# Two layers of sliding-window attention and MLP for one token: adding the quadrants of each head's output once a group instead of once a head

## The chip, the cores and the metric

The kernel runs on 1 core of one Trainium2 chip. The metric is the device time of one execution, in microseconds (us); three runs of the kernel before gave 519.72, 519.97 and 520.18, median 519.97.

## The reference, cut to what matters

Two layers are computed, each with an attention block A and an MLP block B, for one token with D = 640. A has 32 heads of Dh = 192, each with its own keys and values, of which only the last W = 4096 positions count. Both layers read the same caches and weights.

```python
def A(x):
    q = (x @ wq).reshape(1, 1, 32, 192).transpose(0, 2, 1, 3)
    k, v = k_cache[:, :, Sk - W:, :], v_cache[:, :, Sk - W:, :]
    p = softmax(einsum("bhqd,bhkd->bhqk", q, k) * 192 ** -0.5)
    o = einsum("bhqk,bhkd->bhqd", p, v)
    return o.transpose(0, 2, 1, 3).reshape(1, 1, 6144) @ wo
...
x = x + A(layernorm(x))
x = x + B(layernorm(x))     # B: gelu(ln @ w1), shifted, @ w2; gelu(ln @ w3) @ w4
x = x + A(layernorm(x))
x = x + B(layernorm(x))
```

For a single token the shifts of B move in only zeros, so w1 and w2 don't count: B(x) = x + gelu(layernorm(x) @ w3) @ w4.

## The kernel before, in words

A head's K and V are 4096 x 192 bf16, 1.5 MB each, and go into cells: 11 tiles of 12288 bytes on each of 128 partitions. `need(key)` issues, on SyncE's queue (SP), the loads of a fixed order (`layer_stream`) up to the one asked for. Each takes a cell (`take`) that `give` has put back, first in, first out, and its issue waits until the last reader of that cell is done. wq stays in SBUF. Of layer 0's keys, those of heads 0 to 6 stay transposed in cells (NKEEP = 7, `kept`), with the V of head 3 and parts of two others, so that layer 1 need not load them; so the cells that go round become fewer towards the end of layer 0. There w3 and w4 also take cells.

The heads go in 8 groups of 4 (QH); layer 0 from the last group to the first, layer 1 from the first to the last. In `attention`, a group `gi` runs like this:

- K of a head is transposed in four quarters by VectorE in blocks of 32 x 32 words (L377, `T(h, half)` for two quarters), and TensorE forms its scores in two halves (L453, `S(h, half, ...)`).
- The group's softmax is cut into steps (`softmax_steps`): part_max (VectorE), turn_max (TensorE), full_max (VectorE), spread_max (TensorE, then ScalarE's exponential with the row sum), turn_p, swap, recip. Between them stand the transposes and scores of the next group's first two heads, the projection of the q's two groups on (`q[0]` to `q[3]`) and the output projection of the group before (`pending`; either `out_proj`, columns, L597, or `out_row`, rows, L615).
- Then, head by head, `pv` (L569) multiplies V by the probabilities: 16 matmuls write 4 quadrants of PSUM rows, two rows each, with 2 x 192 columns. VectorE turns the result into `o_sb` (L576), an SBUF tile whose bytes also hold the probabilities of the softmax (`o_bytes`).
- Behind each `pv` come the transposes and scores of a later head of the next group, and then `o_fold` (L578 to L589) adds the quadrants: matmuls in fp32 with `Lq` (128 x 32, four unit matrices one below the other) write the head's 192 numbers as 32 x 6, and ScalarE scales them by 1/sum into 32 rows of `oT`. In two groups of layer 1 and four of layer 0, VectorE first adds the two row halves (L587) and one matmul does (L588); in the others two matmuls do (L583). An fp32 matmul shows as two records in the profile.

The next to last group (`hurry`) does the whole softmax of the last group between its own heads. In the last group (`final`), no next group's scores are left: after head 0's `pv` layer 0 projects the `pending` group, then `add_y` adds it; after head 1 `center_y` takes the mean off; the folds of heads 2 and 3 are put off, the one of head 2 into the middle of the next `pv` and that of head 3 behind it. Then the last group is projected and `mixer` (B) follows: two matmuls with `ones` sum the row (L866, L868), w3's columns (L901), gelu, w4's (L933).

`ones` is a 128 x 128 fp32 tile of ones (L264); as the stationary operand of a matmul it adds over partitions and puts the sum on every one (L325, L338, L528, L681, L866, L868). Ahead of the first work on x stand 66 small matmuls into a tile that nobody reads (L308 to L310). All PSUM tiles named psm share a ring of two buffers. The order on TensorE, VectorE, ScalarE and SyncE is that of the program.

Of the kernel before, what the change touches and what calls it, by code (L numbers as in the profile page):

```python
# [17 lines left out]
P = 128  # L18
# [17 lines left out]
def kernel(  # L36
# [37 lines left out]
    NA = Dh // 32  # L74
    NKX = 6
    NKEEP, NCELL = 7, 11
    WARM = 66

# [182 lines left out]
        out=ident[:], in_=ident[:], compare_op=ALU.not_equal, fill=1.0,  # L261
        base=0, pattern=[[-1, P]], channel_multiplier=1,
    )
    ones = const.tile([P, P], F32, name="ones")  # L264
    nc.vector.memset(ones[:], 1.0)
    Lf = wx_sb[:, 0:2 * P].bitcast(F32).rearrange("p (j i) -> p j i", j=4)
    nc.gpsimd.memset(Lf, 0.0)
    for base in (0, -1, -64, -65):
# [20 lines left out]
    blkm = head.tile([P, NM], F32, name="blkm")  # L289
    nc.vector.reduce_sum(blkm[:], ident[:].rearrange("p (m b) -> p m b", m=NM), axis=AX.X)  # L290

    Lq = const.tile([P, 32], F32, name="Lq")
    nc.vector.reduce_sum(Lq[:], ident[:].rearrange("p (j a) -> p a j", j=4), axis=AX.X)
    eps1 = head.tile([P, 1], F32, name="eps1")
    nc.vector.memset(eps1[:], eps)

# [8 lines left out]
    nc.gpsimd.memset(Qblk[:], 0.0)  # L305


    warm_ps = psm.tile([32, 32], F32, tag="psm")  # L308
    for i in range(WARM):
        nc.tensor.matmul(warm_ps[:], lhsT=Eq[:, 0, :], rhs=Eq[:, 0, :], start=(i == 0), stop=(i == WARM - 1))  # L310

    x_rf = wx_sb[0:ND, 6 * P:8 * P].bitcast(F32)
    nc.vector.tensor_copy(x_rf, x_bf)
    xT = const.tile([P, ND], F32, name="xT0")
# [7 lines left out]
    def ln_center(x, rowsum):  # L322

        mean_ps = psm.tile([P, 1], F32, tag="psm")
        nc.tensor.matmul(mean_ps[:], lhsT=ones[:], rhs=rowsum[:, 0:1], start=True, stop=True)  # L325
        xc = big.tile([P, ND], BF16, name="xc")
        nc.vector.scalar_tensor_tensor(out=xc[:], in0=mean_ps[:, 0:1].broadcast_to([P, ND]), scalar=-1.0 / D,
                                       in1=x[:], op0=ALU.mult, op1=ALU.add)
        xcf = big.tile([P, ND], F32, name="xcf")
        nc.vector.scalar_tensor_tensor(out=xcf[:], in0=mean_ps[:, 0:1].broadcast_to([P, ND]), scalar=-1.0 / D,  # L330
                                       in1=x[:], op0=ALU.mult, op1=ALU.add)
        junk = sm.tile([P, ND], F32, tag="ln_junk")
        ssq = sm.tile([P, 1], F32, tag="ln_ssq")
        nc.scalar.activation(junk[:], xcf[:], ACTF.Square, accum_out=ssq[:, 0:1])

        def total():
            var_ps = psm.tile([P, 1], F32, tag="psm")
            nc.tensor.matmul(var_ps[:], lhsT=ones[:], rhs=ssq[:, 0:1], start=True, stop=True)  # L338
            return var_ps

        return xc, xcf, total
# [131 lines left out]
    def softmax_steps(n, ST_ps, sc):  # L473
# [25 lines left out]
        def spread_max():  # L499
            nb_ps = psm.tile([P, 1], F32, tag="psm")  # L500
            nc.tensor.matmul(nb_ps[:], lhsT=held["w"],  # L501
                             rhs=ones[0:1, 0:1], start=True, stop=True)
# [14 lines left out]
        def swap():  # L517
            ng = NGK // NT
            PT_ps = psm.tile([P, n, NJ4, NGK], F32, tag="psm")
            src = held["PrT"].rearrange("p (g j i) -> p i j g", g=ng, j=NJ4)  # L520
            for m in range(NM):
                for q in range(NT):
                    nc.tensor.matmul(PT_ps[32 * m:32 * (m + 1), :, :, ng * q:ng * (q + 1)], lhsT=Eq[:, q, :],  # L523
                                     rhs=src[:, m:QW:NM], start=True, stop=True)
            PT = big.tile([P, n, NJ4 * NGK], BF16, name="PT")
            nc.scalar.copy(PT[:].rearrange("p h c -> p (h c)"), PT_ps[:].rearrange("p h j g -> p (h j g)"))  # L526
            l_ps = psm.tile([P, QH], F32, tag="psm")
            nc.tensor.matmul(l_ps[:], lhsT=ones[:], rhs=held["lh"][:], start=True, stop=True)  # L528
            held["lps"] = l_ps
            return PT  # L530

# [43 lines left out]
            give(("v", layer, h))  # L575
        nc.vector.transpose(o_sb[:], O_ps.rearrange("p (e a c) -> p e c a", e=2, c=NA))  # L576

    def o_fold(h, oT, rl, add=False):  # L578
        r = slice(32 * (h % QH), 32 * (h % QH) + 32)
        oT_ps = psm.tile([P, NA], F32, tag="psm")  # L580
        if not add:
            for e in range(2):
                nc.tensor.matmul(oT_ps[r, :], lhsT=Lq[:], rhs=o_sb[:, e, :, e], start=(e == 0), stop=(e == 1))  # L583
            nc.scalar.activation(oT[r, :], oT_ps[r, :], ACTF.Copy, scale=rl[r, 0:1])  # L584
            return
        o2 = sm.tile([P, NA], F32, name="o2")
        nc.vector.tensor_add(o2[:], o_sb[:, 0, :, 0], o_sb[:, 1, :, 1])  # L587
        nc.tensor.matmul(oT_ps[r, :], lhsT=Lq[:], rhs=o2[:], start=True, stop=True)  # L588
# [52 lines left out]
    def attention(layer, x_cur, rs_cur, x_new, z_new, rs_new, ss_new):  # L641
# [29 lines left out]
        def add_y(y_ps, n):  # L671
            y_new = x_new if n == 0 else sm.tile([P, ND], F32, name="y_acc")
            if n == 1:
# [4 lines left out]

                def center():
                    nm_ps = psm.tile([P, 1], F32, tag="psm")  # L680
                    nc.tensor.matmul(nm_ps[:], lhsT=ones[:], rhs=rs[:, 0:1], start=True, stop=True)  # L681
# [52 lines left out]
        for gi, cur in enumerate(groups):  # L734
            nxt = list(enumerate(groups[gi + 1])) if gi + 1 < len(groups) else []
            ST_n = None
            if nxt:
# [24 lines left out]
                else:  # L762
# [5 lines left out]
                    part_max()  # L768
                    T(h0, 1)
                    S(h0, 0, ST_n, 0)  # L770
                    turn_max()
                    full_max()
                    S(h0, 1, ST_n, 0)
# [32 lines left out]
            hurry = gi + 2 == len(groups)  # L806
            final = gi + 1 == len(groups)
            fold = None
            order = list(enumerate(cur))
# [44 lines left out]
            last = (cur[0] // QH, oT)  # L854
            if not final:
                pending = last
            ST = ST_n
        add_y(out_proj(layer, last) if layer == 0 else out_proj(layer, pending, last), 0)

    def mixer(layer, x_cur, z, rs_cur, ss_cur, x_new, rs_new):  # L860
# [2 lines left out]


        s1_ps = psm.tile([P, 1], F32, tag="psm")
        nc.tensor.matmul(s1_ps[:], lhsT=ones[:], rhs=rs_cur[:, 0:1], start=True, stop=True)  # L866
        s2_ps = psm.tile([P, 1], F32, tag="psm")
        nc.tensor.matmul(s2_ps[:], lhsT=ones[:], rhs=ss_cur[:, 0:1], start=True, stop=True)  # L868
# [119 lines left out]
```

## Time and profile before

| what | value |
|---|---|
| median of three runs | 519.97 us |
| the profiled execution's own time | 519.84 us |
| its span, first to last instruction | 518.0 us |
| TensorE busy (weight loads) | 324.8 us, 63% (192.6 us, 37%) |
| VectorE busy | 295.2 us, 57% |
| ScalarE busy | 49.5 us, 10% |
| read from HBM | 216.47 MB |
| mean TensorE clock granted | 0.70 |
| K transposes, L377 | 228 of 945 ns |
| scores, L453 | 1536 of 380 ns |
| P.V, L569 | 1018 of 461 ns |
| o's transpose, L576 | 64 of 581 ns |

A page of the profile gives, for each engine, the time it was busy, and for each line of the kernel the number of instructions, their busy time, the mean of one, the idle time of the engine right before them and what ended most of it. The timeline gives single instructions by their start. SPq is SyncE's queue of DMA issues; "us to landing" counts from issue until all bytes have arrived. The windows give the same sums for stretches of the span, with the share of TensorE's clock that was granted, the mean busy share of the 16 DMA engines and the bytes moved a second. Busy time of an engine counts only where nothing else is late: the prediction asks for each step what comes last there.

### The profile page before, as it was taken

What the parts mean: (1) busy time and instruction counts of PE and PEld (TensorE: products, weight loads), DVE (VectorE), ACT (ScalarE), POOL (GpSimd) and SP (SyncE); (2) the same over time, 40 slices, a digit from 0 to 9 for tenths busy, and PEclk for the clock granted to TensorE, in tenths of its full rate; (3) what the DMA queues carried; (4) which work ended last, traced back from release to release, by engine and by line L of the source; (5) the groups of instructions that cost most, each with busy time, mean ns of one, the idle gap of its engine ahead of it and who ended that gap; (6) DMA issues with size and microseconds to landing.
All of it is one profiled execution on the core that took longest, in us unless ns stands there. A gap on an engine that the chain in (4) does not pass through costs nothing.

```text
span 518.0 us, 9589 instructions
## 1 busy us (share of the span) xinstructions
PE 324.8 (63%) x4146; PEld 192.6 (37%) x4146; DVE 295.2 (57%) x589; ACT 49.5 (10%) x175; POOL 4.0 (1%) x16
## 2 busy tenths in 40 slices
PE   2057656666664566767755866777566856648665
PEld 2024334333332334434333634434333433425334
DVE  2067667575584655656624356567675765664722
ACT  1000101010010100001011111001010101001011
POOL 2000000000000000000000000000000000000000
PEclk9999878565586755677665778557785676776855
DMA  8999999999999999999999999999999999999995
GB/s 347 433 425 426 433 426 427 432 428 425 433 426 427 431 426 429 428 426 431 424 425 396 385 426 429 428 428 428 429 426 427 432 428 426 426 434 426 427 416 235
DMA packets 23949, 217.08 MB, mean 419 GB/s; under 512 B 2532, under 2 KB 3044, under 8 KB 8420
## 3 DMA queue, kind: packets, MB, share of 16 engines
q1 hardware_dynamic: 23908, 216.48, 99.0%
q8 instruction: 32, 0.52, 0.4%
q14 instruction: 9, 0.07, 0.0%
HBM read 216.47 MB, written 0.00 MB: 418 GB/s over the span
## 4 chain that ended last, share of the span: by engine, by line
DMA 50%; PE 23%; DVE 22%; issue 2%; ACT 1%; SPq 1%; DVEq 0%; ACTq 0%
DMA cell<-in_A_k_cache_dram 39%; DVE cell L377 16%; DMA cell<-in_A_v_cache_dram 9%; PE ST_ps L453 9%; PE O_ps L569 7%; DVE o_sb L576 2%; DMA cell<-in_B_w_dram 2%; DVE pm L478 1%; PE nb_ps L501 1%; DVE o_sb L512 1%; ACT o_sb L507 1%; PE y_ps L637 1%; PE l_ps L528 1%; PE PT_ps L523 1%; PE qT_ps L407 1%
## 5 line engine op out<-in xcount | busy, mean ns | idle before, releaser
L453 PE MATMUL ST_ps<-cell,Qblk 128*16 128x256 bf16 x1536 | 163.7, 380 | 106.9 <-DVE cell L377 69.4
L377 DVE STREAM_TRANSPOSE cell<-cell 128x768 uint32<-128x768 uint32 x228 | 204.1, 945 | 15.2 <-DMA cell<-in_A_k_cache_dram 14.9
L453 PEld LDWEIGHTS <-Qblk 128*16 128x16 bf16 x1536 | 86.1, 111 | 176.5 <-issue 150.3
L569 PE MATMUL O_ps<-cell,PT 128*2 128x384 bf16 x1018 | 99.9, 461 | 8.2 <-DMA cell<-in_A_v_cache_dram 7.4
L576 DVE STREAM_TRANSPOSE o_sb<-O_ps 128x384 f32<-128x384 f32 x64 | 37.2, 581 | 111.8 <-PE O_ps L569 111.6
L569 PEld LDWEIGHTS <-PT 128*2 128x2 bf16 x1024 | 46.0, 100 | 22.1 <-issue 10.1
L512 DVE STREAM_TRANSPOSE o_sb<-o_sb 128x256 bf16<-128x256 bf16 x16 | 7.1, 446 | 33.2 <-ACT o_sb L507 24.2
L584 ACT ACTIVATE oT<-oT_ps,rl 32x6 bf16<-32x6 f32 x40 | 10.3, 258 | 164.0 <-PE oT_ps L583 157.8
L583 PEld LDWEIGHTS oT_ps<-o_sb,Lq 128*32 128x32 f32 x160 | 13.3, 145 | 19.3 <-issue 15.8
L583 PE MATMUL oT_ps<-o_sb,Lq 128*32 128x6 f32 x160 | 13.9, 195 | 10.4 <-DVE o_sb L576 9.9
L589 ACT ACTIVATE oT<-oT_ps,rl 32x6 bf16<-32x6 f32 x24 | 6.2, 258 | 107.6 <-PE ST_ps L453 87.1
L407 PE MATMUL qT_ps<-xc,wq_sb 128*128 128x1 bf16 x210 | 7.1, 165 | 12.8 <-DMA wq_sb<-in_A_wq_dram 12.0
L523 PE MATMUL PT_ps<-o_sb,Eq 128*32 128x32 bf16 x256 | 7.3, 237 | 9.3 <-DVE o_sb L512 4.1
L523 PEld LDWEIGHTS <-Eq 128*32 128x32 bf16 x256 | 5.4, 108 | 19.8 <-issue 19.7
L421 DVE TENSOR_TENSOR Xq<-qT_ps,maskq 128x24 bf16<-128x24 f32 (+1 forms) x18 | 2.8, 158 | 17.1 <-PE qT_ps L407 17.1
L396 PE MATMUL qr_ps<-wq_sb,xc 128*1 128x384 bf16 x90 | 12.1, 415 | 0.0
L407 PEld LDWEIGHTS <-wq_sb 128*128 128x128 bf16 x210 | 6.7, 102 | 14.0 <-DMA wq_sb<-in_A_wq_dram 13.0
L504 ACT COPY nb_sb<-nb_ps 128x1 f32<-128x1 f32 x16 | 2.5, 159 | 94.6 <-PE nb_ps L501 94.6
L615 PE MATMUL yr_ps<-cell,oT 128*1 128x320 bf16 x108 | 11.2, 355 | 0.0
L528 PE MATMUL l_ps<-lh,ones 128*128 128x4 f32 x32 | 7.7, 310 | 4.9 <-ACT PT L526 4.9
L428 PE MATMUL Qrep_ps<-Xq,Lb 128*128 128x24 bf16 (+1 forms) x18 | 3.2, 178 | 11.1 <-DVE Xq L421 10.8
L588 PE MATMUL oT_ps<-o,Lq 128*32 128x6 f32 x48 | 6.1, 199 | 6.5 <-DVE o L587 6.5
(143 smaller groups left out, 200.9 us busy)
## 6 DMA issues: line engine op xcount, KB each, us to landing
cell<-in_A_k_cache_dram SPq DMA_DIRECT2D x57, 1536.0 KB, 26.3
cell<-in_A_v_cache_dram SPq DMA_DIRECT2D x57, 1536.0 KB, 25.8
cell<-in_A_wo_dram SPq DMA_DIRECT2D x13, 960.0 KB, 26.5
wq_sb<-in_A_wq_dram SPq DMA_DIRECT2D x5, 1536.0 KB, 12.2
cell<-in_A_v_cache_dram SPq DMA_DIRECT2D x4, 768.0 KB, 23.8
cell<-in_A_v_cache_dram SPq DMA_DIRECT2D x2, 1248.0 KB, 11.5
cell<-in_B_w_dram SPq DMA_DIRECT2D x1, 1536.0 KB, 11.9
cell<-in_B_w_dram SPq DMA_DIRECT2D x2, 768.0 KB, 10.3
```

What stands on the lines that cost most here:

```text
L377: nc.vector.transpose(Tu, Ku[:, :, q * NY:(q + 1) * NY])
L396: nc.tensor.matmul(qr_ps[32 * i:32 * i + 1, :], lhsT=xc[:, kc:kc + 1], rhs=wq_sb[:, kc, t0 * P + i * N:t0 * P + (i + 1) * N], start=(kc == ...
L407: nc.tensor.matmul(qT_ps[:, tl:tl + 1], lhsT=wq_sb[:, kc, t * P:(t + 1) * P], rhs=xc[:, kc:kc + 1], start=(kc == 0), stop=(kc == ND - 1))
L453: nc.tensor.matmul(ST_ps[r:r + QW, :].rearrange("p (g i) -> p g i", g=ng), lhsT=Q[:, n, :], rhs=T4[:, :, f, :, t], start=(hq == 0 and n == ...
L512: nc.vector.transpose(held["PrT"], held["Pr"])
L523: nc.tensor.matmul(PT_ps[32 * m:32 * (m + 1), :, :, ng * q:ng * (q + 1)], lhsT=Eq[:, q, :], rhs=src[:, m:QW:NM], start=True, stop=True)
L528: nc.tensor.matmul(l_ps[:], lhsT=ones[:], rhs=held["lh"][:], start=True, stop=True)
L569: nc.tensor.matmul(O_ps[r:r + 2, :], lhsT=PT[:, hq, 2 * i:2 * i + 2], rhs=v_pair(V, h, 2 * i * Dh, 2 * Dh), start=(i < 4), stop=(i >= NB - 4))
L576: nc.vector.transpose(o_sb[:], O_ps.rearrange("p (e a c) -> p e c a", e=2, c=NA))
L583: nc.tensor.matmul(oT_ps[r, :], lhsT=Lq[:], rhs=o_sb[:, e, :, e], start=(e == 0), stop=(e == 1))
L584: nc.scalar.activation(oT[r, :], oT_ps[r, :], ACTF.Copy, scale=rl[r, 0:1])
L615: nc.tensor.matmul(yr_ps[32 * i:32 * i + 1, :], lhsT=oT[:, k:k + 1], rhs=wo_t[:, k * D + i * N:k * D + (i + 1) * N], start=(k == 0), stop= ...
```

## The change

- In all groups but the last of each layer, VectorE adds the two row halves of every head right behind o's transpose (`o_add`), into a row block of `o4` (128 x 4 x 6). `o_fold` is no longer called there.
- One fp32 matmul a group (`group_fold`), with `L4` (four copies of `Lq` side by side, 128 x 128), adds the quadrants of all four heads and puts each head's numbers on all four blocks of rows; four ScalarE activations scale them into `oT`. It stands in the next group behind the first half of its first head's scores (`pending_fold`), and for the next to last group behind the first P.V of the last one.
- In layer 0's last group the projection of the pending group moves from behind head 0's P.V to behind head 1's, and `center_y` from behind head 1's to behind head 2's. The last group of each layer keeps `o_fold`, with two matmuls a head.
- `ones` becomes a column of ones, read with step 0 as 128 x 128.
- The 66 matmuls at the start go, and `L4` takes four reductions at the start instead of one.

```diff
-    WARM = 66
...
-    ones = const.tile([P, P], F32, name="ones")
-    nc.vector.memset(ones[:], 1.0)
+    one = const.tile([P, 1], F32, name="one")
+    nc.vector.memset(one[:], 1.0)
+    ones = one[:, 0:1].broadcast_to([P, P])
...
-    Lq = const.tile([P, 32], F32, name="Lq")
-    nc.vector.reduce_sum(Lq[:], ident[:].rearrange("p (j a) -> p a j", j=4), axis=AX.X)
+    L4 = const.tile([P, P], F32, name="L4")
+    Lq = L4[:, 0:32]
+    for j in range(4):
+        nc.vector.reduce_sum(L4[:, 32 * j:32 * j + 32], ident[:].rearrange("p (j a) -> p a j", j=4), axis=AX.X)
...
-    warm_ps = psm.tile([32, 32], F32, tag="psm")
-    for i in range(WARM):
-        nc.tensor.matmul(warm_ps[:], lhsT=Eq[:, 0, :], rhs=Eq[:, 0, :], start=(i == 0), stop=(i == WARM - 1))
...
-    def o_fold(h, oT, rl, add=False):
+    def o_fold(h, oT, rl):
         r = slice(32 * (h % QH), 32 * (h % QH) + 32)
         oT_ps = psm.tile([P, NA], F32, tag="psm")
-        if not add:
-            for e in range(2):
-                nc.tensor.matmul(oT_ps[r, :], lhsT=Lq[:], rhs=o_sb[:, e, :, e], start=(e == 0), stop=(e == 1))
-            nc.scalar.activation(oT[r, :], oT_ps[r, :], ACTF.Copy, scale=rl[r, 0:1])
-            return
-        o2 = sm.tile([P, NA], F32, name="o2")
-        nc.vector.tensor_add(o2[:], o_sb[:, 0, :, 0], o_sb[:, 1, :, 1])
-        nc.tensor.matmul(oT_ps[r, :], lhsT=Lq[:], rhs=o2[:], start=True, stop=True)
+        for e in range(2):
+            nc.tensor.matmul(oT_ps[r, :], lhsT=Lq, rhs=o_sb[:, e, :, e], start=(e == 0), stop=(e == 1))
         nc.scalar.activation(oT[r, :], oT_ps[r, :], ACTF.Copy, scale=rl[r, 0:1])
+
+    def o_add(h, o4):
+        nc.vector.tensor_add(o4[:, h % QH, :], o_sb[:, 0, :, 0], o_sb[:, 1, :, 1])
+
+    def group_fold(o4, oT, rl):
+        oT_ps = psm.tile([P, QH, NA], F32, tag="psm")
+        nc.tensor.matmul(oT_ps[:].rearrange("p h c -> p (h c)"), lhsT=L4[:], rhs=o4[:].rearrange("p h c -> p (h c)"),
+                         start=True, stop=True)
+        for i in range(QH):
+            r = slice(32 * i, 32 * i + 32)
+            nc.scalar.activation(oT[r, :], oT_ps[r, i, :], ACTF.Copy, scale=rl[r, 0:1])
...
                     S(h0, 0, ST_n, 0)
+                    if pending is not None:
+                        pending_fold()
                     turn_max()
...
                 pv(layer, h, hq, PT, fold)
+                if not final:
+                    o_add(h, o4)
                 if final:
-                    if layer == 0 and hq == 0:
+                    if hq == 0:
+                        pending_fold()
+                    if layer == 0 and hq == 1:
                         add_y(out_proj(layer, pending), 1)
-                    if hq == 1:
+                    if hq == 2 - layer:
                         center_y()
...
-                o_fold(h, oT, rl, len(groups) - 4 > gi >= 2 * layer)
                 if hurry and hq == 3:
...
                 pending = last
+
+                def pending_fold(o4=o4, oT=oT, rl=rl):
+                    group_fold(o4, oT, rl)
```

More of the change, by code (lines that the diff above doesn't have):

```diff
@@ L324, in ln_center @@
         mean_ps = psm.tile([P, 1], F32, tag="psm")
-        nc.tensor.matmul(mean_ps[:], lhsT=ones[:], rhs=rowsum[:, 0:1], start=True, stop=True)
+        nc.tensor.matmul(mean_ps[:], lhsT=ones, rhs=rowsum[:, 0:1], start=True, stop=True)
         xc = big.tile([P, ND], BF16, name="xc")
@@ L337, in total @@
             var_ps = psm.tile([P, 1], F32, tag="psm")
-            nc.tensor.matmul(var_ps[:], lhsT=ones[:], rhs=ssq[:, 0:1], start=True, stop=True)
+            nc.tensor.matmul(var_ps[:], lhsT=ones, rhs=ssq[:, 0:1], start=True, stop=True)
             return var_ps
@@ L501, in spread_max @@
             nc.tensor.matmul(nb_ps[:], lhsT=held["w"],
-                             rhs=ones[0:1, 0:1], start=True, stop=True)
+                             rhs=one[0:1, 0:1], start=True, stop=True)
             nb_sb = big.tile([P, 1], F32, name="nb_sb")
@@ L527, in swap @@
             l_ps = psm.tile([P, QH], F32, tag="psm")
-            nc.tensor.matmul(l_ps[:], lhsT=ones[:], rhs=held["lh"][:], start=True, stop=True)
+            nc.tensor.matmul(l_ps[:], lhsT=ones, rhs=held["lh"][:], start=True, stop=True)
             held["lps"] = l_ps
@@ L680, in center @@
                     nm_ps = psm.tile([P, 1], F32, tag="psm")
-                    nc.tensor.matmul(nm_ps[:], lhsT=ones[:], rhs=rs[:, 0:1], start=True, stop=True)
+                    nc.tensor.matmul(nm_ps[:], lhsT=ones, rhs=rs[:, 0:1], start=True, stop=True)
                     ym = big.tile([P, ND], F32, name="y_m")
@@ L808, in attention @@
             fold = None
+            o4 = None if final else big.tile([P, QH, NA], F32, name="o4")
             order = list(enumerate(cur))
@@ L865, in mixer @@
         s1_ps = psm.tile([P, 1], F32, tag="psm")
-        nc.tensor.matmul(s1_ps[:], lhsT=ones[:], rhs=rs_cur[:, 0:1], start=True, stop=True)
+        nc.tensor.matmul(s1_ps[:], lhsT=ones, rhs=rs_cur[:, 0:1], start=True, stop=True)
         s2_ps = psm.tile([P, 1], F32, tag="psm")
-        nc.tensor.matmul(s2_ps[:], lhsT=ones[:], rhs=ss_cur[:, 0:1], start=True, stop=True)
+        nc.tensor.matmul(s2_ps[:], lhsT=ones, rhs=ss_cur[:, 0:1], start=True, stop=True)
         def centred(dt, name):
```

## The prediction

> **What bounds the kernel now.** I read the page's line of DMA share first, then the rate by stretches, then the chain of waits, then the timeline where the rate falls.
>
> The page, busy tenths in 40 slices of 12.95 us, and the queue's share:
>
> ```profile
> DMA  8999999999999999999999999999999999999995
> ...
> q1 hardware_dynamic: 23908, 216.48, 99.0%
> ...
> DMA 50%; PE 23%; DVE 22%; issue 2%; ACT 1%; SPq 1%; DVEq 0%; ACTq 0%
> ```
>
> Every slice but the first and the last is 9: the loads' queue is busy 99.0% of the span, TensorE 63% and VectorE 57%. The chain names PE and DVE for 45%, but it follows a load back to what let it be issued, even if the load then stood behind others, so I don't price edits by it. I take four stretches of the table of windows (columns: length, busy time of PE, weight loads, DVE, ACT, POOL; granted clock; DMA share; GB/s):
>
> ```profile
> 4.00:270.00 266.00, 161.79 (x1888) 93.96 (x1889) 155.57 (x292) 21.59 (x75) 0.00 (x0) 0.72 1.01 428
> 270.00:300.00 30.00, 19.70 (x442) 13.93 (x442) 11.59 (x46) 3.90 (x18) 0.00 (x0) 0.63 0.99 395
> 300.00:490.00 190.00, 127.07 (x1531) 73.21 (x1527) 120.22 (x213) 18.14 (x63) 0.71 (x2) 0.69 1.01 428
> 490.00:518.00 28.00, 16.28 (x291) 11.48 (x291) 7.55 (x37) 4.58 (x19) 0.00 (x0) 0.57 0.81 332
> ```
>
> 456 of the 518 us run at 428 GB/s, and 217.08 MB at 428 take 507.2 us. The other 10.8 us are the start (4 us at 169 GB/s: 2.4 lost), the change of layers (30 x (1 - 395/428) = 2.3 lost) and the end (28 x (1 - 332/428) = 6.3 lost). Nothing done in the two long stretches shortens them; a change can gain at most in the last three.
>
> At the change of layers the queue runs nearly dry twice, at 282 to 286 and at 292 to 296:
>
> ```profile
> 282.00:284.00 2.00, 1.98 (x62) 1.90 (x62) 0.88 (x8) 0.58 (x3) 0.00 (x0) 0.50 0.86 340
> 284.00:286.00 2.00, 0.71 (x27) 0.81 (x28) 1.44 (x10) 1.30 (x6) 0.00 (x0) 0.50 0.94 307
> 292.00:294.00 2.00, 2.00 (x58) 1.30 (x47) 0.15 (x1) 0.46 (x2) 0.00 (x0) 0.91 1.03 340
> 294.00:296.00 2.00, 1.65 (x54) 1.22 (x54) 0.83 (x3) 0.00 (x0) 0.00 (x0) 1.00 0.84 301
> ```
>
> By the same sum they lose 1.0 us each. There the next loads wait for cells that a chain of small steps frees: last V lands (277.06), P.V, o folded, y, mixer (w3's cell free 283.69, w4's about 287), q and scores of layer 1 (first kept cell free 291.01).
>
> **The change, part by part.** The profiled execution took 519.84 us (span 518.0 and 1.84 around it), 0.13 below the median 519.97.
>
> *The folds of 14 groups (seven a layer).* Rows of the groups:
>
> ```profile
> L583 PE MATMUL oT_ps<-o_sb,Lq 128*32 128x6 f32 x160 | 13.9, 195 | 10.4 <-DVE o_sb L576 9.9
> L588 PE MATMUL oT_ps<-o,Lq 128*32 128x6 f32 x48 | 6.1, 199 | 6.5 <-DVE o L587 6.5
> L528 PE MATMUL l_ps<-lh,ones 128*128 128x4 f32 x32 | 7.7, 310 | 4.9 <-ACT PT L526 4.9
> ```
>
> Gone: 128 of the 160 matmuls of L583 (32 heads x 4; the last groups' 8 heads keep theirs), 128 x 0.195 = 25.0 us by single durations (overlapped, 13.9 x 0.8 = 11.1 busy), and all of L588, 6.1 busy. Added: one fp32 matmul a group, two records like L528's, which take 0.59 us together at half clock: 14 x 0.59 = 8.3. TensorE is 9 us less busy. VectorE gets 56 - 24 = 32 more adds of 0.149 us (L587) = 4.8 us, all standing between o's transpose and the next head's K transposes. ScalarE keeps 64 activations, four in a row per group (4 x 0.258 = 1.03 us). They stand ahead of nb_sb's copy, which waits anyway for the second half of scores.
>
> On the compute path a head loses its fold between scores and P.V (0.35 to 0.6 us) and gains 0.15 on VectorE; the group end loses TensorE's wait of 0.78 us for o_sb, and the next group's T is late there instead. The group fold comes after the first half of scores, where TensorE waits for the second half's K transposes (two of 0.945 us and part_max's 0.39 against 1.45 us of scores): the cover is about 0.8 us for 0.59, and without it softmax starts some 0.3 us later. So each group's compute is 1 to 2 us shorter, and this buys nothing, because the groups are paced by landings: 0. If the queue weren't full it would be worth up to 14 x 2 us; the 428 GB/s of the stretches rule that out.
>
> *The pending projection of layer 0's last group moves one head back, and this frees a cell later.* Following takes and gives of the cells: V of head 3, the last V of the layer, sat in the cell that the pending out_proj frees; now it takes head 1's V cell, and w3 gets the projection's. The timeline (SPq rows are issues; in brackets what ended the wait):
>
> ```profile
> 264.45 0.96 PE L597 MATMUL y_ps<-oT,cell 128*128 128x1 bf16 x30
> 264.56 1.28 SPq L145 DMA_DIRECT2D cell<-in_A_v_cache_dram  x3
> ...
> 267.40 1.45 PE L569 MATMUL O_ps<-cell,PT 128*2 128x384 bf16 x16 [1.68 <-DMA cell<-in_A_v_cache_dram]
> ...
> 268.89 0.39 SPq L177 DMA_DIRECT2D cell<-in_B_w_dram  x1
> ...
> 277.06 0.81 PE L569 MATMUL O_ps<-cell,PT 128*2 128x384 bf16 x8 [2.85 <-DMA cell<-in_A_v_cache_dram]
> ```
>
> V 3 was issued by 265.8; now it waits for head 1's P.V, which a landing holds at 267.40, and goes at 268.89 where w3 went; w3, queued on SP behind it, about 1 us later, when the projection ends. Is 268.89 too late? The four wq loads that TensorE waits for arrive at 10.63, 14.29, 17.99 and 21.63, 3.67 us apart. So the first, issued at 0.75 into an empty queue, landed near 6.97: 6.2 us from issue, 3.67 of streaming and 2.5 fixed. V 3 lands at 277.06, so an issue up to 270.9 holds it: 2.0 us to spare. Taken: 0; bound +0.7 (the sixteen engines don't run level, and the rate already sags a little at 271).
>
> The group fold there (0.59) and four activations stand behind head 0's P.V; TensorE then waits 1.68 us for V 1. The projection and its add go where it waits 1.98 us for V 2; center_y where it waits 2.85 us for V 3. In layer 1's last group the fold is covered downstream by waits for loads of 0.61, 0.58, 0.23 and 0.89 us up to w3's second half at 511.10; if they were gone it would cost 0.6.
>
> *ones becomes one column read 128 times with step 0.* No row shows such a weight load. Nearest: L866's 128x128 fp32 load, 0.31 us. Below it could cost as little as L483's load (0.08), above I allow twice, so -0.23 to +0.31 a load. Between 277 and 291 two matmuls (s1 and mean, two loads each) lie on the chain that frees cells: -0.9 to +1.2 us. Still 128 columns are loaded, so I take 0. At the end w3's landing hides it.
>
> *No warm-up.* 66 matmuls, 1.9 us at 4.28, with TensorE waiting for wq until 21.63: 0. The first scores at 27.13 took 1.44 us per half, exactly as at 307.71 where the granted clock was 0.50; so the warm-up had left nothing. The Trainium skill ("TensorE: Matmul & The Clock Gate", Why this matters for your kernels) speaks against removing it: 4 us of matmuls keep the array at full clock. By that rule the first scores would be slower without it; the same page's idle window of 3.4 us agrees with the row that they are already slow.
>
> *Setup:* three more reductions of 0.37 us on VectorE ahead of x's cast, which waits 1.08 for x: xc may be ready 0.1 later, and wq's last chunk comes 12 us after. 0.
>
> Sum: 519.84 + 0 = 519.8; the runs' median lies 0.1 higher, so **519.9**.
>
> **Rivals.**
> 1. *Faster through the change of layers.* If the clock there (0.50 until about 292.4) is granted a stretch earlier, the scores of heads 0 and 1 take 0.86 (row at 292.71) instead of 1.46 us each, cells come 1.2 us earlier and the second dip's 1.0 us goes: 518.8. A cheap step-0 load does the same. Against: the change adds hardly any TensorE work between 277 and 292. 12 in 100.
> 2. *Slower: V 3 comes late.* Its issue now hangs on head 1's P.V. From 270.9 on each us is a us on everything after; 0.2% needs 272.0, that is head 1's P.V ending 3.1 us later than now, or step 0 and skew working together. Price then as a dip of today, 1.0 to 1.3: 521.1. 8 in 100.
> 3. *Slower: the step-0 weight load* at twice the price, +1.2 us of chain: 521.1. 6 in 100.
> 4. *The change doesn't free the compute path*, since T takes the place of each fold: also 519.9, inside the forecast.
>
> **How the numbers follow.** About 0.2% (1.04 us) is what a measurement of this kernel tells from no change. Forecast 74 in 100, rival 1 12, rivals 2 and 3 together 14. The bounds -1.0 and +1.2 about 519.9 give 518.8 to 521.1. Faster 0.12, within 0.74, slower 0.14.
>
> **What would show it.** Right: 428 GB/s in both long stretches; SP's issue of V 3 near 268.9 and its P.V still near 277; no wait of TensorE for o_sb at group ends, the same time for T; loads issued earlier after their cells. Wrong: a third dip at 270 to 275; s1 and mean longer than 0.59 us; the clock at full before 290; a rate that isn't 428 when the engines touch memory less.

## The result, and the profile after

| | median | runs | lowest to highest |
|---|---|---|---|
| before | 520.17 us | 22 | 519.52 to 521.96 |
| after | 521.21 us | 22 | 519.75 to 524.64 |

The ratio is 1.0024, 95% interval 1.0014 to 1.0033: slower by 0.24%, 1.0 us. Forecast were 519.9, no change, and 518.8 to 521.1 as bounds. The profiled execution took 521.01 us (span 519.2), 1.2 more than before's.

The page and the table of windows of the kernel after (columns as in the prediction):

```profile
DMA  8999999999999999999999999999999999999995
...
q1 hardware_dynamic: 23908, 216.48, 98.9%
```

```profile
4.00:270.00 266.00, 161.88 (x1753) 89.20 (x1755) 158.83 (x305) 21.57 (x75) 0.00 (x0) 0.71 1.01 428
270.00:300.00 30.00, 20.59 (x436) 14.38 (x434) 11.44 (x48) 3.74 (x17) 0.00 (x0) 0.59 1.00 389
300.00:490.00 190.00, 123.57 (x1440) 69.46 (x1440) 123.61 (x232) 17.50 (x60) 0.71 (x2) 0.69 1.01 428
490.00:519.00 29.00, 17.22 (x306) 11.90 (x306) 8.35 (x41) 5.35 (x22) 0.00 (x0) 0.60 0.81 330
```

Both long stretches still run at 428 GB/s. TensorE's busy time fell by 1.5 us (324.8 to 323.3) and not by the forecast 9: the folds' own rows fell from 20.0 to 11.3 us, but those of P.V rose from 99.9 to 106.1. VectorE's rose from 295.2 to 302.4. The loss is in the change of layers (389 instead of 395) and at the end.

**A third dip.** The 3 us from 270, and the dip of 282 to 286 (340 and 307 GB/s before), in windows of before and then of after:

```profile
270.00:273.00 3.00, 1.04 (x10) 0.23 (x10) 1.02 (x2) 0.26 (x1) 0.00 (x0) 0.50 1.04 431
```

```profile
270.00:273.00 3.00, 1.08 (x14) 0.37 (x13) 0.97 (x4) 0.26 (x1) 0.00 (x0) 0.50 0.91 326
...
282.00:284.00 2.00, 2.00 (x56) 2.00 (x57) 0.89 (x8) 0.53 (x3) 0.00 (x0) 0.50 1.04 412
284.00:286.00 2.00, 0.70 (x27) 0.71 (x25) 1.19 (x8) 1.02 (x5) 0.00 (x0) 0.50 1.10 389
```

326 instead of 431 GB/s is a hole in the stream of loads, the third dip that the prediction named as a sign of being wrong. The old dip behind it, at 282 to 286, has become shallower: part of what the queue would have lost there is already lost at 271. The timeline of after shows who came late:

```profile
264.65 4.75 SPq L144 DMA_DIRECT2D cell<-in_A_v_cache_dram  x3
...
267.58 1.45 PE L567 MATMUL O_ps<-cell,PT 128*2 128x384 bf16 x16 [1.91 <-DMA cell<-in_A_v_cache_dram]
268.96 0.96 PE L600 MATMUL y_ps<-oT,cell 128*128 128x1 bf16 x30
...
269.95 0.39 SPq L176 DMA_DIRECT2D cell<-in_B_w_dram  x1
...
277.51 0.81 PE L567 MATMUL O_ps<-cell,PT 128*2 128x384 bf16 x8 [2.60 <-DMA cell<-in_A_v_cache_dram]
```

V 3 is the V of head 3, the last V of layer 0; V 1 and V 2 are those ahead of it. The row at 264.65 holds three issues; the third, V 3, ends with it at 269.40, behind head 1's P.V, as predicted (268.89). Its P.V starts at 277.51 instead of 277.06.

**Waits that moved.** TensorE's waits over the whole span (us in total, times, longest), first of before, then of after:

```profile
PE ST_ps L453 <- DVE cell L377: 69.4, 76, 3.8
PE ST_ps L453 <- DVE pm L478: 32.3, 13, 4.2
...
PE oT_ps L583 <- DVE o_sb L576: 9.9, 13, 0.8
...
PE oT_ps L588 <- DVE o L587: 6.5, 9, 1.0
```

```profile
PE ST_ps L451 <- DVE cell L375: 78.7, 88, 3.7
PE ST_ps L451 <- DVE pm L476: 41.9, 13, 4.8
```

The folds' 16.4 us of waits are gone, and the scores wait 18.9 us longer for VectorE's transposes and its part_max. So the folds stood where TensorE had to wait anyway.

**Room that shrank.** Compute has room while it stands waiting for loads: if it gets slower by less than that wait, the loads still set the time. How long VectorE's K transposes waited for keys to land is one measure of it. Their row in before and in after, each first over the whole span and then for 300 to 490 us, in layer 1 (busy, mean ns, idle before it and what ended it):

```profile
L377 DVE STREAM_TRANSPOSE cell<-cell 128x768 uint32<-128x768 uint32 x228 | 204.1, 945 | 15.2 <-DMA cell<-in_A_k_cache_dram 14.9
...
L377 DVE STREAM_TRANSPOSE cell<-cell 128x768 uint32<-128x768 uint32 x100 | 89.4, 944 | 3.1 <-DMA cell<-in_A_k_cache_dram 3.0
```

```profile
L375 DVE STREAM_TRANSPOSE cell<-cell 128x768 uint32<-128x768 uint32 x228 | 204.7, 947 | 6.6 <-DMA cell<-in_A_k_cache_dram 6.4
...
L375 DVE STREAM_TRANSPOSE cell<-cell 128x768 uint32<-128x768 uint32 x100 | 89.9, 947 | 1.0 <-DMA cell<-in_A_k_cache_dram 0.9
```

15.2 us of waiting for loads have become 6.6, and 3.1 have become 1.0 in layer 1: the kernel after computes more slowly, not faster.

### The profile page after: what moved, and what is told of

Read it like the earlier page. It is cut to its first block, busy times and chain, and to the rows that moved or that the text cites. A ratio compares the mean times of both kernels' runs of the same rounds, so it can differ in the third digit from the quotient of the medians.

```text
span 519.2 us, 9181 instructions
## 1 busy us (share of the span) xinstructions
PE 323.3 (62%) x3932; PEld 184.9 (36%) x3932; DVE 302.4 (58%) x624; ACT 49.4 (10%) x175; POOL 4.0 (1%) x16
## 4 chain that ended last, share of the span: by engine, by line
DMA 33%; PE 31%; DVE 29%; issue 4%; ACT 2%; SPq 1%; DVEq 0%; ACTq 0%
DVE cell L375 21%; DMA cell<-in_A_k_cache_dram 20%; PE ST_ps L451 12%; PE O_ps L567 9%; DMA cell<-in_A_v_cache_dram 8%; DVE o_sb L574 3%; DMA cell<-in_B_w_dram 2%; DMA kx<-in_A_v_cache_dram 2%; PE qr_ps L394 1%; PE nb_ps L499 1%; PE yr_ps L618 1%; PE l_ps L526 1%; DVE pm L476 1%; PE y_ps L640 1%; PE PT_ps L521 1%
## 5 line engine op out<-in xcount | busy, mean ns | idle before, releaser
L451 PE MATMUL ST_ps<-cell,Qblk 128*16 128x256 bf16 x1536 | 157.9, 371 | 121.9 <-DVE cell L375 78.7
L451 PEld LDWEIGHTS <-Qblk 128*16 128x16 bf16 x1536 | 82.7, 110 | 200.1 <-issue 171.7
L567 PE MATMUL O_ps<-cell,PT 128*2 128x384 bf16 x1018 | 106.1, 465 | 10.4 <-DMA cell<-in_A_v_cache_dram 8.3
L618 PE MATMUL yr_ps<-cell,oT 128*1 128x320 bf16 x108 | 13.7, 413 | 0.0
L526 PE MATMUL l_ps<-lh,one 128*128 128x4 f32 x32 | 8.2, 326 | 4.9 <-ACT PT L524 4.9
L584 DVE TENSOR_TENSOR o<-o_sb 128x6 f32<-128x6 f32 x56 | 9.4, 169 | 1.9
L499 PE MATMUL nb_ps<-one,o_sb 1*128 1x1 f32 x32 | 8.3, 326 | 3.5 <-DVE o_sb L491 3.5
L499 PEld LDWEIGHTS nb_ps<-one,o_sb 1*128 1x128 f32 x32 | 7.0, 269 | 9.9 <-issue 5.0
L526 PEld LDWEIGHTS l_ps<-lh,one 128*128 128x128 f32 x32 | 6.8, 264 | 7.5 <-ACT PT L524 7.1
L505 ACT ACTIVATE o_sb<-ST_ps,nb_sb,sc 128x256 bf16<-128x256 f32 x16 | 9.0, 565 | 0.5
```

What stands on the lines that cost most here:

```text
L451: nc.tensor.matmul(ST_ps[r:r + QW, :].rearrange("p (g i) -> p g i", g=ng), lhsT=Q[:, n, :], rhs=T4[:, :, f, :, t], start=(hq == 0 and n == ...
L499: nc.tensor.matmul(nb_ps[:], lhsT=held["w"], rhs=one[0:1, 0:1], start=True, stop=True)
L526: nc.tensor.matmul(l_ps[:], lhsT=ones, rhs=held["lh"][:], start=True, stop=True)
L567: nc.tensor.matmul(O_ps[r:r + 2, :], lhsT=PT[:, hq, 2 * i:2 * i + 2], rhs=v_pair(V, h, 2 * i * Dh, 2 * Dh), start=(i < 4), stop=(i >= NB - 4))
L584: nc.vector.tensor_add(o4[:, h % QH, :], o_sb[:, 0, :, 0], o_sb[:, 1, :, 1])
L618: nc.tensor.matmul(yr_ps[32 * i:32 * i + 1, :], lhsT=oT[:, k:k + 1], rhs=wo_t[:, k * D + i * N:k * D + (i + 1) * N], start=(k == 0), stop= ...
```

## The experiments

Theory A: V 3 is late and the queue runs dry. Rival B: the folds, adds, ones or the missing warm-up cost. Rival C: the loss arises at the end of the kernel by itself. Later rivals: D, both together; E, compute has room to spare. Each run was timed beside the kernel before on the same chip. For each profiled run the table gives V 3's issue and the MB still queued then; the arrears at 276 and at 490 us (time less what the bytes moved so far by the loads' queue take at 428 GB/s, summed from the trace's packets); VectorE's wait for keys over the whole span; the start of the last group's softmax (first weight load for PT_ps, 1.5 us ahead of the matmuls); and the end of the span. The starts in the expectations are in the same measure. Ratios and intervals are those of all runs of a kernel; medians are named where they tell something else.

| run | V 3 issued, MB left | arrears 276, 490 | K wait | last softmax, end | ratio, interval |
|---|---|---|---|---|---|
| before | 265.8, 2.44 | 3.2, 6.1 | 15.2 | 491.7, 518.0 | 1 |
| after | 269.4, 0.94 | 4.2, 6.7 | 6.6 | 493.4, 519.2 | 1.0024, 1.0014 to 1.0033 |
| r_after | 269.2, 0.99 | 4.4, 6.4 | 6.5 | 495.8, 518.6 | 1.0013, 1.0000 to 1.0026 |
| e1 | 267.4, 1.74 | 3.2, 6.2 | 6.1 | 493.8, 519.3 | 1.0000, 0.9991 to 1.0009 |
| e1_again | 267.3, 1.75 | 3.1, 6.1 | 7.5 | 492.9, 518.6 | 1.0009, 0.9996 to 1.0023 |
| e2 | 269.2, 1.02 | 4.6, 6.7 | 16.5 | 492.8, 519.0 | 1.0007, 0.9998 to 1.0015 |
| e2_again | 269.2, 0.98 | 4.0, 6.4 | 15.4 | 492.5, 518.9 | 1.0007, 0.9997 to 1.0017 |
| e3 | 266.5, 2.24 | 4.4, 6.9 | 7.6 | 500.7, 523.7 | 1.0016, 0.9998 to 1.0033 |
| e4 | 265.8, 2.39 | 3.2, 6.0 | 19.3 | 492.0, 517.6 | 0.9999, 0.9989 to 1.0009 |
| e5 | 266.1, 2.34 | 4.0, 6.4 | 6.8 | 498.8, 522.0 | 1.0032, 1.0015 to 1.0049 |
| e6 | 270.1, 0.66 | 3.9, 6.3 | 21.5 | 492.2, 517.9 | 1.0003, 0.9994 to 1.0013 |
| e7 | 267.2, 1.84 | 3.2, 6.1 | 13.9 | 490.7, 517.8 | 1.0006, 0.9995 to 1.0016 |
| e8 | 265.7, 2.41 | 3.2, 6.1 | 8.9 | 499.5, 522.3 | 1.0025, 1.0010 to 1.0040 |
| e9 | 269.4, 0.92 | 4.2, 6.9 | 12.8 | 491.7, 519.3 | 1.0011, 1.0002 to 1.0021 |
| f1 | 269.4, 0.87 | 4.1, 6.8 | 7.8 | 494.2, 518.5 | 1.0010, 0.9996 to 1.0025 |
| f2 | 269.2, 0.93 | 3.8, 6.4 | 12.0 | 491.5, 518.8 | 1.0008, 0.9999 to 1.0016 |
| f3 | 269.6, 0.86 | 4.1, 6.8 | 11.7 | 496.6, 519.0 | 1.0014, 1.0006 to 1.0023 |
| f4 | 265.8, 2.41 | 3.1, 6.3 | 14.1 | 498.1, 520.9 | 1.0071, 1.0054 to 1.0088 |

The column of K waits is mostly layer 0. Between 300 and 490 us it is 3.1 in before, 1.0 and 0.1 in after and r_after, 0.1 in e1, e3, e5, f1 and in e8, f3 and f4 (whose added work stands in layer 1 alone, so that their column shows nothing of it), 1.0 in e1_again, 1.5 and 1.6 in e7 and f2, 3.9 in e9, and 5.8 to 7.1 in e2, e2_again, e4 and e6.

**e1, the projection back.** In the kernel after (layer 0's last group):

```diff
-                    if layer == 0 and hq == 1:
+                    if layer == 0 and hq == 0:
...
-                    if hq == 2 - layer:
+                    if hq == 1:
```

> The kernel after, with the projection of the last group of layer 0 put back behind head 0's P.V (and center_y behind head 1's); the group's fold and its four activations now stand right ahead of it. Theory A (the late issue of V 3 is the cause): the projection frees its cell about 1.6 us later than in the kernel before (fold 0.6, activations 1.0), so V 3 is issued near 267.3 instead of 269.4; the dip at 270 to 272 is gone or under 0.3 us, and the time falls by 0.5 to 1.0 us against the kernel after, to 520.2 to 520.7. Rival B (the folds and adds of the other groups, or ones with step 0, are the cause): the time stays at 521.2, whatever V 3 does. Rival C (the extra microsecond arises at the end of the kernel, from a late w3 or a hiccup there): the time stays at 521.2 and the span to 490 is that of before.

V 3 went at 267.38 and the hole is gone. Windows of e1:

```profile
270.00:273.00 3.00, 1.04 (x11) 0.23 (x10) 1.02 (x2) 0.26 (x1) 0.00 (x0) 0.50 1.03 434
```

The time was that of before (520.08 against 519.99). As A has it; B and C expected 521.2.

**e2, only the projection moved.** e1's edit the other way round, in the kernel before.

> The kernel before, with one thing changed: the pending projection of the last group of layer 0 goes behind head 1's P.V and center_y behind head 2's in layer 0, head 1's in layer 1, as in the kernel after. All folds, ones and the warm-up as before. Theory A: V 3 is issued near 269 instead of 265.8, the rate falls to 260 to 350 GB/s between 270 and 272, and the time rises by 0.5 to 1.0 us to 520.7 to 521.2. Rivals B and C: no dip of importance, 520.2 as before.

The hole is there (308 GB/s from 270 to 273), the median rose by 0.2 us, ratio 1.0007 with an interval that holds 1: the sign of A, but too little for the whole of it.

**e3, the last two groups as before.** In the kernel after:

```diff
-            o4 = None if final else big.tile([P, QH, NA], F32, name="o4")
+            o4 = None if final or hurry else big.tile([P, QH, NA], F32, name="o4")
...
+                if hurry:
+                    o_fold(h, oT, rl)
```

and e1's edit, without `pending_fold` in the last group.

> The kernel after, with the last two groups of each layer as before: the next-to-last group folds each head by itself (two matmuls, without the add), the projection and center_y are back at their old places. Group folds and adds stay in the first six groups of each layer, ones has step 0, no warm-up. Theory A: V 3 is issued near 265.8, no dip at 270, and the time is that of before, 520.2 (within 0.4). Rival B: 521.2, since nearly all folds and adds, ones and the missing warm-up are still there. Rival C: between, with the loss after 490.

V 3 was early, and the median, 520.35, is within A's 0.4 of before; but three of twelve runs took over 522 us, the ratio is 1.0016, and the trace, of one of the long runs, ends at 523.7. No theory had foreseen that. Two things in it were new. V 2 was issued at 265.56 with 1.08 MB left (before: 264.89, 1.27), since the softmax ahead of it ended later, and the rate fell to 332 GB/s from 267 to 270. And at the end the last products no longer wait for loads. Timeline of before, then of e3:

```profile
502.59 0.81 PE L569 MATMUL O_ps<-cell,PT 128*2 128x384 bf16 x8 [0.61 <-DMA cell<-in_A_v_cache_dram]
...
506.11 0.56 PE L597 MATMUL y_ps<-oT,cell 128*128 128x1 bf16 x15 [0.58 <-DMA cell<-in_A_wo_dram]
```

```profile
510.10 0.81 PE L567 MATMUL O_ps<-cell,PT 128*2 128x384 bf16 x8 [0.69 <-DVE o_sb L574]
...
512.79 1.76 PE L600 MATMUL y_ps<-oT,cell 128*128 128x1 bf16 x60
```

In before a V ends the wait; in e3 VectorE does, and the 60 columns of the projection run in one piece: the compute path had fallen 9 us behind and set the end.

**e4, ones and warm-up alone.** In the kernel before:

```diff
-    ones = const.tile([P, P], F32, name="ones")
-    nc.vector.memset(ones[:], 1.0)
+    one = const.tile([P, 1], F32, name="one")
+    nc.vector.memset(one[:], 1.0)
+    ones = one[:, 0:1].broadcast_to([P, P])
...
-    for i in range(WARM):
-        nc.tensor.matmul(warm_ps[:], lhsT=Eq[:, 0, :], rhs=Eq[:, 0, :], start=(i == 0), stop=(i == WARM - 1))
```

> The kernel before with only two things of the change: ones is one column read with step 0, and there is no warm-up; all folds as before. Theory A: 520.2 as before (within 0.3), s1 and mean at 0.59 us, first scores at 1.44 us per half. Rival B in the form that step 0 or the missing warm-up costs: 520.7 to 521.2.

0.9999: together they cost nothing that the interval, 0.5 us each way, would show. s1 takes 0.59 us and the first scores 1.44, as expected.

**r_after and e2_again**, unchanged, on one chip.

> The kernel after once more, unchanged, beside the next three on one chip: e1 gave the time of before (ratio 1.0000), e2 with the same late V 3 only 1.0007, after 1.0024. Theory A (one mechanism: the queue runs dry at 270 because V 3 is issued with 0.9 to 1.0 MB left in it; 0.9 us are lost there, about 0.5 stay): after and e2 have the same true price, 0.4 to 0.8 us, and come out within 0.4 us of each other here. Rival D (the late V 3 costs more together with the group folds): after again 0.9 to 1.2 us over before, e2 under 0.4.

> The kernel before with only the projection and center_y moved, as in e2, once more on the same chip as the kernel after. Theory A: 0.4 to 0.8 us over before, within 0.4 us of the kernel after. Rival D: under 0.4 over before, at least 0.5 under the kernel after.

0.67 us over before for after (1.0013); for e2 0.36 by the ratio and 0.70 by the medians. They lie at most 0.3 apart, within A's 0.4 and within the intervals, so D isn't shown; but by the ratio e2 came out at 0.36 both times, just under A's range.

**e5, the fold earlier**, in the kernel after, with e1's edit:

```diff
-                    if hq == 0:
-                        pending_fold()
...
                 if hurry and hq == 3:
-                    for step in steps[2:5]:
+                    steps[2]()
+                    group_fold(o4, oT, rl)
+                    for step in steps[3:5]:
```

> The kernel after, but in the next-to-last group of each layer the group's fold stands at its own end, between full_max and spread_max of the last group's softmax, and so the projection and center_y can stand at their old places right behind head 0's P.V. Theory A: V 3 is issued right behind V 2 again (0.5 us later), so no dip of its own; but the fold now delays head 0's P.V and with it V 2. If V 2 is issued before 265.3 (more than 1.15 MB left), the time is that of before; if at 265.4 to 265.8, the queue runs dry at 267 by 0.2 to 0.7 us, and half of it stays: 520.1 to 520.4. Rival D: the folds cost by themselves, 0.5 or more over before.

V 2 went at 265.16 with 1.16 MB left, and the arrears rose by 0.5 already by 270. But the time, 1.0032, is far over what A allows, and the last softmax started at 498.8. Like e3, this is a compute path that sets the end: behind 498 us TensorE waits for no load in either trace. Theory A by itself had failed.

**e6, V 3 still later.** e2, and head 1's cell is given back behind the projection:

```diff
-        else:
+        elif not hold:
             give(("v", layer, h))
...
+                    if hold:
                         add_y(out_proj(layer, pending), 1)
+                        give(("v", layer, h))
```

> A second dose of the late issue: e2, but head 1's V cell is given back after the projection, so V 3 takes the projection's cell and is issued near 270.3 instead of 269.3, with about 0.6 MB left in the queue instead of 1.0. All folds as before. Theory A: the hole at 270 to 272 grows by the same 0.9 to 1.0 us, to about 2.0 us; V 3's P.V starts about 1 us later than in e2, and the chain that frees the next cells with it, so 1.2 to 1.8 us over before: 521.2 to 521.8. If the queue's level is not what matters, e6 equals e2.

V 3 went 0.9 us later, and the hole was no larger than in e2 and e2_again (308 and 360 GB/s), nor was the time (1.0003; A expected at least 1.2 us). Windows of e6:

```profile
270.00:273.00 3.00, 1.09 (x11) 0.23 (x10) 1.04 (x2) 0.26 (x1) 0.00 (x0) 0.50 0.96 359
```

So the size of the hole doesn't follow from the MB left. Here w3 followed at once (0.5 us; 0.9 in e2); whether that is why stays open.

**e7 and e9, folds and adds off the compute path.** In the kernel after; e7 has e1's edit too:

```diff
-                if not final:
-                    o_add(h, o4)
...
+                o_add(h, o4)
                 if hurry and hq == 3:
...
                     T(h0, 1)
+                    if pending is not None:
+                        pending_fold()
                     S(h0, 0, ST_n, 0)
-                    if pending is not None:
-                        pending_fold()
                     turn_max()
```

> The kernel after, with the group fold and the adds moved off the compute path and the projection back behind head 0's P.V: o's add is issued on VectorE behind the next head's four K transposes (where the kernel before has its add), and the group's fold stands ahead of the first half of scores, where TensorE waits for VectorE anyway. Theory A+B (late V 3 costs about 0.4 us through the queue; the folds cost by a slower compute path, which at the end of the kernel lies just behind the loads): three heads in a row take at most 16.6 us again instead of 17.07 where the clock is half, the last group's PT_ps matmuls start near 492 instead of 493.4 to 495.8, and the time is that of before, ratio 0.999 to 1.0005, with no run over 522. Rival E (compute lies far behind the loads and only V 3 matters): also the time of before, but equal to e1's in spread and in the last group's start as well.

> The kernel after with adds and folds moved off the compute path as in the run before it, but the projection left where the kernel after has it, so that V 3 is late. Theory A+B: only the price of the late V 3 is left: ratio 1.0005 to 1.001 (0.3 to 0.5 us), with no run over 522. Rival E: the same as the kernel after, 1.0013 to 1.0024.

The room is back (13.9 and 12.8 us of waiting for keys, last softmax 490.7 and 491.7, three heads at most 16.6 us), and no run went over 521.5. The times, 1.0006 and 1.0011, lie a little over the expected ranges, and by them neither kernel can be told from the other, nor e7 from before. The traces are as A with B has it; the times are too close to show it.

**e8, the room measured.** In e4:

```diff
+                if layer == 1 and not final:
+                    for i in range(2):
+                        nc.vector.tensor_add(od[:, i, :], o_sb[:, 0, :, 0], o_sb[:, 1, :, 1])
```

> Measures how much room the compute path has at the end. The kernel before (ones with step 0 and no warm-up, as e4, which gave 0.9999), and behind each head's transpose of o in the first seven groups of layer 1 two adds of o's quadrants into a tile that nobody reads, 0.15 us each, ahead of the next K transposes: twice what the kernel after puts there. Theory A+B: the heads get 0.3 us longer each, the last group's PT_ps matmuls start 4 to 8 us later than 492, that is at 496 to 500, and since in the traces with a late start (498.8 and 500.7) the kernel ended 23 us after it, the time rises by 1 to 5 us to 521 to 525. Rival E: the loads still set the end, 0 to 0.2 us.

> The kernel after with only the projection put back (e1), once more beside the three others. Theory A+B: V 3 costs nothing here, the slower compute path costs now and then: ratio 1.0000 to 1.0010, single runs up to 523. Rival E: 1.0000 and no long runs.

0.62 us of useless adds in three heads (17.23 instead of 16.61) cost 1.0025, at the foot of the expected range, with 4 of 12 runs over 522: E is out. In e8's trace, too, TensorE waits for no load behind 498 us. e1_again, 1.0009 with one run at 523.62, goes with it.

**f1 to f4, which half, and does it add up.** f1 moves only the adds as in e7, f2 only the fold; f3 is e8 with e2's edit; f4 is e8 with `range(4)`.

> The kernel after with only the adds moved off the compute path (o's add behind the next head's K transposes); the group's fold and the late projection stay. If the adds take most of the room: three heads at most 16.6 us, group turns 13.0 to 13.6 as after, last group's PT_ps start 492 to 494, ratio 1.0005 to 1.0015. If the fold inside the softmax takes it: last start 495 or later in a slow profile and ratio as the kernel after, 1.0013 to 1.0024, with runs over 522.

> The kernel after with only the group's fold moved ahead of the first half of scores; the adds stay right behind o's transpose, the projection stays late. If the adds take most of the room: three heads up to 17.07 us, last start 493 to 496, ratio as the kernel after, 1.0013 to 1.0024, with runs over 522. If the fold takes it: last start 492 to 493.5, ratio 1.0005 to 1.0012, no run over 522.

> e8 (two useless adds a head in layer 1) with the projection of layer 0's last group moved as in e2, so that V 3 is late as well. If the two prices add up: e8's 1.0025 and e2's 0.0007 give 1.0032 (within 0.001). If a late V 3 sharpens the lag (the whole of layer 1 starts 0.5 us later on a path without room): 1.0045 or more. If they hide each other, as two chains of which only the longer counts: 1.0025.

> e8 with four useless adds a head instead of two. e8's two adds lengthened three heads from 16.61 to 17.23 us (0.1 us each add) and brought the last group's PT_ps start from 492.0 to 499.5 for a median of plus 1.0 us. If the compute path's room ends at a start near 495 and counts one to one beyond it: three heads near 17.9, start 504 to 508, time plus 6 to 11 us (526 to 531). If the loads still set the end for the most part: plus 1 to 3 us.

With the fold left inside the softmax (f1) the wait for keys stays at 7.8 and one run took 523.81; with the fold moved (f2) it is 12.0 and none passed 521.3. Both take room: three heads take 16.61 us in f1 and 17.07 in f2. By these waits the fold's place takes the larger share, but that is one trace each, and at half clock the two cost about the same (below). By times they can't be told apart. f3 (1.0014, none of 11 runs over 522) missed all three forecasts and lies below e8 (1.0025), though the intervals overlap: nothing shows that late V 3 and lag sharpen each other. f4 (3.4 to 3.7 us) missed both forecasts, 6 to 11 and 1 to 3: four adds lengthened three heads to 17.5 at most and not 17.9.

## Why the prediction was wrong, point by point

**The bound: right.** 428 GB/s in both long stretches of all traces (427 in the first of e3 and e5, whose V 2 was late).

**V 3: the step that failed first.** "An issue up to 270.9 holds it: 2.0 us to spare" was worked out from V 3's last byte in a queue taken as one stream. The issue came at 269.40, and the queue ran dry. By the packets, the sixteen engines are some 3.3 us apart in the list of loads: in before the first packet of V 3 (12288 bytes) starts at 269.7, and the last of V 2 (4608 bytes) ends at 273.0. In after V 3's first packet starts at 270.7; V 2's go on until 273.2, while from 271 to 272 the rate is already down to 318 GB/s. So the first engine sets the deadline, not the mean. Over all traces: issues with 1.20 MB (2.8 us at 428) or more still queued cost at most 0.2 us, V 2's with 1.16 and 1.08 (e5, e3) 0.5 and 0.9 by 270 (arrears against before), and V 3's with 0.66 to 1.02 made the holes here. How large a hole gets doesn't follow from that number alone (e6). The nine traces with a late V 3 have arrears of 3.8 to 4.6 us at 276, the seven with neither V 2 nor V 3 late 3.1 to 3.2: 1.0 us is lost. At 490 it is 6.6 on average against 6.1: half is given back in the next dip, which waits for cells and not for the queue. The price is then 0.5 us by the traces, and 0.16 to 0.36 by the ratios of e6 and e2 (0.2 to 0.7 by their medians); the prediction had a bound of 0.7 and took 0. Rival 2 had the right place, but its point, 272.0, lay 2.6 us behind the issue that already cost.

**The folds: wrong in sign.** "Each group's compute is 1 to 2 us shorter" failed in both its parts. The removed matmuls stood where TensorE waits for K transposes anyway. And the cover of 0.8 us for the group's fold isn't there: behind part_max TensorE runs without a gap up to spread_max. A turn of before, and one of after at the same clock (first half 1.45 us in both):

```profile
402.58 1.45 PE L453 MATMUL ST_ps<-cell,Qblk 128*16 128x256 bf16 x12 [1.72 <-DVE pm L478]
403.96 0.37 PE L483 MATMUL pmT_ps<-ident,pm 128*1 128x128 f32 x1
404.26 1.50 PE L453 MATMUL ST_ps<-cell,Qblk 128*16 128x256 bf16 x12
```

```profile
434.37 1.45 PE L451 MATMUL ST_ps<-cell,Qblk 128*16 128x256 bf16 x12 [2.93 <-DVE pm L476]
435.75 0.62 PE L588 MATMUL oT_ps<-o,L 128*128 128x24 f32 x2
436.19 0.39 PE L481 MATMUL pmT_ps<-ident,pm 128*1 128x128 f32 x1
436.51 1.38 PE L451 MATMUL ST_ps<-cell,Qblk 128*16 128x256 bf16 x12
```

From the first half's start to the second's it is 1.68 us in before and 2.14 in after: 0.46 a group. The add, ahead of the next K transposes, makes three heads 17.07 us at half clock instead of 16.61 (from the first of a group's o transposes to the fourth), 0.15 a head, just its price.

"And this buys nothing, because the groups are paced by landings" is true only while there is room. In the traces whose last softmax starts at 498 or later the span ends 22.8 to 23.2 us behind that start (e3, e5, e8, f4); before ends at 518.0, so its room goes up to about 495.2, and it starts at 491.7: 3.5 us. After starts at 493.4 and 495.8: 1.8 and none. Its two traces show the difference: in the first TensorE still waits 0.95 us for w3 at 511.96, and in r_after it waits for no load behind 498 us and the span ends 22.8 us behind the start. So it costs in some runs and not in others: of the kernels with the group's fold inside the softmax (after, r_after, e1, e1_again, e3, e5, f1) 15 of 92 runs took over 522 us; of before 0 of 156 (the slowest 521.96), of those without that fold and without added lag (e2, e2_again, e4, e6, e7, e9, f2) 0 of 82. That the long runs of after itself are of this kind is inferred from e3, e5 and e8, whose traces are of such runs; after has no trace of one. The edit worked out as a gain was the one that took the room.

**What the two make together.** Late V 3 without group folds 1.0003 to 1.0007, group folds without late V 3 1.0000 and 1.0009, both 1.0013 and 1.0024. The first measurement of after lies above the sum; whether by chance stays open, as f3 speaks against a sharpening. In the profiled run 0.5 of the 1.2 us are arrears; the other 0.7 arise behind 490, where the traces whose loads set the end scatter by more (511.6 to 513.1 us for end less arrears). They are no lag of compute, as TensorE's wait for w3 ends at 511.96 instead of 511.10 there; in e1 it ends at 512.22 with hardly more arrears than before has. Why w3 lands later by more than the arrears stays open.

**ones with step 0: right, 0.** s1 and mean take 0.59 us as before, and e4 gives 0.9999. Rival 3 is out. **No warm-up: right, 0**, by e4 too; the 66 matmuls ran 1.9 us, so that the 4 us held against their removal did not apply to them. **Setup: right:** in after TensorE still waits for wq, 1.79 us for the second part of it.

**Rival 1, the clock at the change of layers: no gain.** Full clock came at 292.4 in before and 294.3 in after. In all traces the turn there, from layer 0's last o transpose to layer 1's first, takes 24.7 to 26.0 us where full clock starts by 294.7, 26.5 to 26.9 at 298.7 to 299.1, and 28.4 to 28.6 at 301.9 to 302.2 (r_after, e3, e5): up to 3.8 us of room hang on when the clock rises. The clock records change in steps of 3.41 us. The Trainium skill ("TensorE: Matmul & The Clock Gate", Part 1) says that activity is judged in free-running windows of about 3.4 us, so that the moment of a change varies from run to run; the records here agree.

## What to carry to other kernels

In a kernel bound by its loads, first measure how far compute is ahead, by how long the first consumer of the loads still waits for them, and look for the place where that room is smallest; an edit that took half of it here cost in some runs only. A matmul that fills a wait is free, and taking it out buys nothing; the same work put on a chain without gaps is paid in full, so ask what the engine does on both sides of the new place. A load is on time when the first of the sixteen engines gets it in time; here issues with 2.8 us of queue ahead of them were, and with 2.7 us or less they were not.

## What the runs showed of the hardware

- Behind a queue of 2.4 MB one load's first packet started 3.3 us before the last of the load ahead of it ended (269.7 and 273.0 in before). The Trainium skill ("DMA: Bandwidth & Descriptors", Queues, rings and completion order) says that each engine consumes its own ring in order; the packets here, which don't name their engine, fit it.
- The share of busy time shows such a hole only in part: from 270 to 273 it fell from 1.04 to 0.91 while the rate fell from 431 to 326 GB/s. V 3's first packets took up to 2.07 us in after instead of 0.46, and count as busy all the while: in r_after the microsecond from 271 moved 287 GB/s at a share of 1.00 (each packet spread evenly over its time).
- A weight load of one column with step 0 costs what a full 128 x 128 fp32 tile does: 0.59 us for the two records of s1.
